# Slot tiles placed at multiples of 512 bytes in a decode kernel (attention over a long cache and an MLP)

## The chip, the cores and the metric

The kernel runs on one core of a Trainium2 chip. The metric is the device time of one execution in microseconds (us); the time before is a median of 404.12 us over three runs (403.59 to 404.19). The profile is that of one execution.

## What is computed

One token, a vector `x` of 1,024 numbers, goes through two branches that both start from the same layer norm; their results and `x` are added. Everything is bfloat16 in memory.

```python
xn = _layernorm(x)
return x + A(xn, k_cache, v_cache, wq, wo) + B(xn, w1, w2, w3, w4)

def A(x, k_cache, v_cache, wq, wo):        # caches: 4 heads x 65536 keys x 128
    q = (x @ wq) as 32 heads of 128        # 8 query heads share one cache head
    scores = q @ k.T * 128 ** -0.5
    return (softmax(scores) @ v) as one row @ wo

def B(x, w1, w2, w3, w4):
    h = gelu(layernorm(x) @ w1)
    hs = (h, each quarter shifted along the tokens) @ w2
    x1 = x + hs
    return x1 + gelu(layernorm(x1) @ w3) @ w4
```

With one token the shifted `h` is zero throughout, so that `x1` is `x`. The work is to read 134 MB of caches and 36 MB of weights once.

## The kernel before, in words

**Slots.** All the large data passes through three buffers of the pool `big` (L69, `SLOTS = 3`), each one tile `slot` of 128 partitions by 32,768 bf16 numbers, which is 65,536 bytes in each partition and 8.39 MB in all. The list `slots` (L112 to L123) sets the order of the stream: `wq`; then for each of the four cache heads `g` and each of its two blocks `t` one slot of keys (K) and one of values (V); `w3` behind the first V; a slot with `w1`, the first piece of `w4` and some gathered rows of `w4` ahead of the last head; `wo`; and last `w2` with the three remaining pieces of `w4` (`W4_PIECES = (13, 9, 3, 1)` rows a partition). So there are 21 slots of data for three buffers.

**The queue.** `issue` (L155) takes the next buffer and starts its transfers from SyncE (SP) at L169, one DMA for each piece. Each partition's part of a piece is contiguous both in HBM and in SBUF, so a DMA of a whole slot is 128 runs of 65,536 bytes, eight for each of 16 DMA engines. The main loop (L543) calls `ensure(i + LOOKAHEAD)` with `LOOKAHEAD = 2`: before slot `i` is worked on, slot `i + 2` is issued, which waits on SP until the buffer that it takes, that of slot `i - 1`, has been read for the last time. The gathered rows (L162 to L164) come through the GpSimd queue.

**Work on a slot.** A slot of keys (`compute_K`, L421) is done in two halves of 16,384 keys. For each half VectorE transposes the tile in place in four steps (L430, 128x2048 float32 words each), and TensorE multiplies it with the query held in `qst` (L434, 32 matmuls), followed by a running maximum (L438), the exponential (L457) and a transpose of the probabilities (L471). A slot of values (`compute_V`, L474) is 64 matmuls (L481) and two updates of the accumulator `og`. The weights go straight into matmuls of one row (L317, L525, L226). At the end ScalarE copies the sum `psB` out (L412), and SP writes it to HBM (L413).

**Where tiles lie in SBUF.** Pools lie one behind the other in the order in which they are opened (L66 to L71): `const`, `small`, `one`, `big`, `pp`, `tp`. Every tile is rounded up to 32 bytes. In the built program's table of allocations 16,384 bytes of each partition are reserved, four small constants follow, and `const` begins at byte 16,512. The three small pools take 9,664 bytes, so that the three slots begin at bytes 26,176, 91,712 and 157,248. Each of these is 64 more than a multiple of 512 (26,176 = 51 x 512 + 64). Pieces that share a slot begin at multiples of 2,048 bytes within it, so that every piece begins at 64 past a multiple of 512 too. `pp` begins at 222,784 and `tp` at 224,832. Among the tiles of `const` are `qst` and `eps_t`, the constant 1e-5 that the layer norm's square root takes as its bias (L201, L249).

Of the kernel before, what the change touches and what calls it, by code (L numbers as in the profile page):

```python
# [9 lines left out]
F32 = mybir.dt.float32  # L10
# [5 lines left out]
SLOTS = 3  # L16
# [7 lines left out]
XR = (4, 1)  # L24
XP = (((0, 12), (16, 20), (28, 44), (48, 52), (60, 68), (92, 100), (124, 128)), ((68, 84), (100, 116)))
NO_ROW = 4096


@with_exitstack
def kernel(  # L30
# [15 lines left out]
    P = 128  # L46
# [16 lines left out]
    assert FW <= 512 and F % 8 == 0  # L63
    SCALE = float(DH) ** -0.5

    const = ctx.enter_context(tc.tile_pool(name="const", bufs=1))  # L66
    small = ctx.enter_context(tc.tile_pool(name="small", bufs=2))
    one = ctx.enter_context(tc.tile_pool(name="one", bufs=1))
    big = ctx.enter_context(tc.tile_pool(name="big", bufs=SLOTS))  # L69
    ppool = ctx.enter_context(tc.tile_pool(name="pp", bufs=1))  # L70
    tpool = ctx.enter_context(tc.tile_pool(name="tp", bufs=2))  # L71
    dram = ctx.enter_context(tc.tile_pool(name="dram", bufs=1, space=bass.MemoryType.DRAM))
# [60 lines left out]
    def fill_x_row():  # L133
# [4 lines left out]
        for i, r in enumerate(XR):  # L138
            row, step = tmp(1), tmp(1)
            nc.vector.tensor_scalar(out=row, in0=pf, scalar1=float(x_start[i] // r + NO_ROW), scalar2=None, op0=ALU.add)  # L140
            end = 0
            for a, b in XP[i]:
                for t, jump in ((a, -NO_ROW - (a - end)), (b, NO_ROW)):
                    nc.vector.tensor_scalar(out=step, in0=pf, scalar1=float(t), scalar2=float(jump),
# [53 lines left out]
    make_identity(nc, ident_bf)  # L198
    ident_f = const.tile([P, P], F32, name="ident_f")
    make_identity(nc, ident_f[:])  # L200
    eps_t = const.tile([P, 1], F32, name="eps_t")  # L201
    nc.gpsimd.memset(eps_t[:], LN_EPS)
    ones_f = early[:, 64:192]
    nc.gpsimd.memset(ones_f, 1.0)
# [4 lines left out]
    def tmp(w):  # L209
        n_tmp[0] += w  # L210
        assert n_tmp[0] <= 512
        return early[:, n_tmp[0] - w:n_tmp[0]]
# [368 lines left out]
```

## Time and profile before

| | |
|---|---|
| median of three runs | 404.12 us (403.59 to 404.19) |
| profiled execution, its own time | 402.96 us |
| its span, from first to last instruction | 401.2 us |
| mean granted TensorE clock | 0.836 of full speed |
| busy: DMA queue of SP / VectorE / TensorE / ScalarE | 98% / 54% / 53% / 9% |
| bytes moved by DMA | 170.1 MB in the records, 170.67 MB read from HBM |

Busy time is the share of the span in which an engine ran instructions; for the DMA queue it is the time that its packets took, as a share of 16 engines' span. A *packet* is here one record of the trace, one contiguous run of bytes moved by one DMA engine. The profile's chain of waits follows the work that ended last back from the end: at each step to what released it. The groups give, for instructions of one kind, their number, total and mean duration, and the idle time of their engine ahead of them with the releaser. GB/s in the 40 slices of the span jumps between 410 and 460 because a packet's bytes are booked whole; the mean is what counts.

### The profile page before, as it was taken

The page shows a single profiled execution, that of the slowest core. Times are in us where ns is not written, and L with a number is a line of the kernel's source. Part 1 is how long each engine was busy: PE and PEld are TensorE (multiplying, and loading weights), DVE is VectorE, ACT ScalarE, POOL GpSimd, SP SyncE. Part 2 cuts the span into 40 slices and gives each one's busy share as a digit, 9 for nine tenths or more (in the row PEclk, how much of TensorE's full clock was granted, in tenths as well). Part 3 has the DMA queues.
Part 4 walks back from the last instruction along what each step waited for, and adds up shares of the span by engine and source line. Part 5 has one row for each costly group of instructions (what it writes and reads, how often), then busy time and mean ns, then how long its engine had stood idle before and what let it go on. Part 6 is the DMA issues. An engine that isn't in the chain of part 4 may idle for free.

```text
span 401.2 us, 3446 instructions
## 1 busy us (share of the span) xinstructions
PE 210.8 (53%) x1452; PEld 86.3 (22%) x1452; DVE 218.0 (54%) x291; ACT 35.7 (9%) x62; POOL 14.7 (4%) x24
## 2 busy tenths in 40 slices
PE   0003868540885196419662953385801965295763
PEld 0001323220332032104230411132400422031221
DVE  0006299501986498339845972696503982497300
ACT  0001000510012001100110011002200021001100
POOL 3000000002000000000000005100000000000000
PEclk9999969995798689958985999599865898599667
DMA  9999999999999999999999999999999999999985
GB/s 379 457 418 419 418 420 452 463 427 419 425 418 433 418 451 459 418 425 412 446 425 464 433 418 418 435 440 396 452 418 464 438 425 426 418 431 426 464 379 211
DMA packets 4234, 170.10 MB, mean 424 GB/s; under 512 B 936, under 2 KB 948, under 8 KB 1220
## 3 DMA queue, kind: packets, MB, share of 16 engines
q1 hardware_dynamic: 3608, 169.35, 98.0%
q0 software_dynamic: 416, 0.54, 0.4%
q8 instruction: 11, 0.18, 0.2%
q10 hardware_dynamic: 196, 0.00, 0.0%
q14 instruction: 3, 0.02, 0.0%
HBM read 170.67 MB, written 0.01 MB: 425 GB/s over the span
## 4 chain that ended last, share of the span: by engine, by line
DMA 54%; DVE 32%; PE 10%; another core or an unknown queue 2%; ACT 1%; ACTq 1%; issue 1%; SPq 0%; DVEq 0%
DMA slot<-in_A_k_cache_dram 38%; DVE slot L430 27%; DMA x_row_bf<-in_A_x_dram 9%; DMA slot<-in_B_w_dram 7%; PE oacc L481 4%; PE sc L434 3%; DVE mx L438 3%; PE rows L317 2%; DVE pT L471 1%; PE psB L226 1%; DVE og L489 1%; ACTq L180 1%; PE pm_mx L447 0%; DVE qst L330 0%
## 5 line engine op out<-in xcount | busy, mean ns | idle before, releaser
L434 PE MATMUL sc<-slot,qst 128*128 128x512 bf16 x512 | 133.7, 412 | 105.3 <-DVE slot L430 105.3
L430 DVE STREAM_TRANSPOSE slot<-slot 128x2048 f32<-128x2048 f32 x64 | 142.9, 2280 | 68.7 <-DMA slot<-in_A_k_cache_dram 68.6
L434 PEld LDWEIGHTS <-qst 128*128 128x128 bf16 x512 | 51.5, 103 | 175.6 <-DMA slot<-in_A_k_cache_dram 59.9
L481 PE MATMUL oacc<-slot,pT 128*32 128x512 bf16 x512 | 38.3, 452 | 6.8 <-DVE og L489 3.2
L457 ACT ACTIVATE p_sb<-sc,nm 128x1024 bf16<-128x1024 f32 x16 | 17.8, 1114 | 184.8 <-DVE nm L454 120.4
L471 DVE STREAM_TRANSPOSE pT<-p_sb 128x1024 bf16<-128x1024 bf16 x16 | 19.9, 1244 | 17.3 <-ACT p_sb L457 17.3
L438 DVE TENSOR_REDUCE mx<-sc 128x1 f32<-128x1024 f32 x16 | 19.2, 1203 | 4.5 <-PE sc L434 4.4
L481 PEld LDWEIGHTS <-pT 128*32 128x32 bf16 x512 | 14.8, 109 | 23.8 <-issue 12.0
L489 DVE SCALAR_TENSOR_TENSOR og<-og,alpha,oacc 128x512 f32<-128x512 f32 x12 | 8.8, 735 | 19.2 <-PE oacc L481 19.2
L238 PE MATMUL pm_ln<-early 128*128 128x1 f32 x4 | 1.1, 356 | 33.2 <-DVE early L274 30.7
L232 DVE CAST early<-x_bf 128x8 f32<-128x8 bf16 x1 | 0.2, 171 | 29.0 <-DMA x_bf<-in_A_x_dram 29.0
L440 PE MATMUL pm_mx<-ident_f,mx 128*1 128x128 f32 x16 | 4.3, 270 | 15.9 <-DVE mx L438 15.9
L457 ACT ACT_TABLE_LOAD x3 | 3.8, 1283 | 92.0 <-DVE nm L452 58.4
L162 POOL MEMSET slot<- 128x5120 bf16 x1 | 4.4, 4364 | 146.8 <-PE oacc L481 146.8
L238 PEld LDWEIGHTS pm_ln<-early 128*128 128x128 f32 x4 | 1.0, 313 | 33.2 <-issue 30.6
L447 PE MATMUL pm_mx<-ident_f,rep 1*128 1x1 f32 x16 | 3.6, 226 | 8.1 <-DVE rep L444 8.1
L525 PE MATMUL pm_w<-slot,oT 128*1 128x512 bf16 x64 | 5.7, 538 | 3.4 <-DMA slot<-in_A_wo_dram 3.4
L504 PE MATMUL pm_e<-og,sel8q 128*32 128x128 f32 x32 | 4.2, 276 | 5.0 <-DVE og L496 5.0
L317 PE MATMUL rows<-slot,early 128*32 128x512 bf16 x64 | 6.4, 589 | 0.0
L447 PEld LDWEIGHTS pm_mx<-ident_f,rep 1*128 1x128 f32 x16 | 2.3, 142 | 18.2 <-DVE rep L444 18.2
L440 PEld LDWEIGHTS pm_mx<-ident_f,mx 128*1 128x1 f32 x16 | 1.3, 79 | 21.3 <-DVE mx L438 20.4
L317 PE MATMUL rows<-slot,xpad 128*32 128x448 bf16 (+1 forms) x80 | 5.5, 358 | 0.0
(101 smaller groups left out, 95.4 us busy)
## 6 DMA issues: line engine op xcount, KB each, us to landing
slot<-in_B_w_dram SPq DMA_DIRECT2D x1, 7168.0 KB, 31.0
slot<-in_B_w_dram SPq DMA_DIRECT2D x2, 2048.0 KB, 28.4
slot<-in_B_w_dram SPq DMA_DIRECT2D x1, 3328.0 KB
slot<-in_B_w_dram SPq DMA_DIRECT2D x1, 2304.0 KB, 27.2
slot<-in_B_w_dram SPq DMA_DIRECT2D x1, 768.0 KB
slot<-in_B_w_dram SPq DMA_DIRECT2D x1, 256.0 KB
slot<-in_A_k_cache_dram SPq DMA_DIRECT2D x8, 48.2
slot<-in_A_v_cache_dram SPq DMA_DIRECT2D x8, 37.3
```

The costliest lines, as they stand in the source:

```text
L162: nc.gpsimd.memset(loaded[piece], 0.0)
L317: nc.tensor.matmul(acc[32 * j:32 * j + 32, bk, 0:width], lhsT=xp[:, c, :], rhs=wt[:, cl, ch * width:(ch + 1) * width], start=(c == 0), sto ...
L430: nc.vector.transpose(out=kf[:, cg, :], in_=kf[:, cg, :])
L434: nc.tensor.matmul(sc[:, hf, :], lhsT=qst[:, o:o + 128], rhs=kr[:, cg, hf, :, bp // 2, :, bp % 2], start=(cg == 0 and bp == 0), stop=(cg = ...
L438: nc.vector.reduce_max(out=mx[:], in_=sc[:].rearrange("p h n -> p (h n)"), axis=AX.X)
L440: nc.tensor.transpose(pm[0:1, 0:P], mx[:, 0:1], ident_f[:])
L447: nc.tensor.transpose(pm[:, P:P + 1], rep[0:1, :], ident_f[0:1, 0:1])
L457: nc.scalar.activation(out=p_sb[:], in_=sc[:], func=ACTF.Exp, bias=nm[:, 0:1], scale=SCALE, accum_out=lb[:, 0:1])
L471: nc.vector.transpose(out=pT[:], in_=p_sb[:])
L481: nc.tensor.matmul(oacc[32 * u:32 * (u + 1), :], lhsT=pT[:, hf, 32 * t:32 * (t + 1)], rhs=vt[:, :, hf, t, :], start=(hf == 0 and t < 4), s ...
L489: nc.vector.scalar_tensor_tensor(out=st["og"][:], in0=st["og"][:], scalar=alpha[:, 0:1], in1=oacc[:], op0=ALU.mult, op1=ALU.add)
L525: nc.tensor.matmul(psW[32 * q:32 * q + 1, :], lhsT=lhsT, rhs=wrow[:, 512 * b:512 * b + 512], start=(i < 2), stop=(i >= n - 2), tile_positi ...
```

## The change

Two pools are opened ahead of `const`: a new pool `head` with a single tile, and the pool `big`, which stood behind `one`. The tile in `head` is 96 float32 numbers, 384 bytes in a partition; its first number takes the part of `eps_t`, which leaves `const`. With that the tile begins at byte 16,512 = 32 x 512 + 128, and the first slot 384 bytes later, at 16,896 = 33 x 512. As a slot is 128 x 512 bytes, the other two begin at multiples of 512 as well (82,432 and 147,968), and so does every piece in them. The small pools follow at 213,504 = 417 x 512. As `eps_t` with its 32 bytes is gone from `const`, the tiles behind it move by 32 bytes against their pool's start: `qst`, which began at a multiple of 64, begins at 32 past one, and so do the tiles of `pp` and `tp` (now from 223,136 and 225,184).

No instruction is added, removed or given another shape, and the order in which they are issued stays.

```diff
+HEAD = 96
...
+    head = ctx.enter_context(tc.tile_pool(name="head", bufs=1))
+    big = ctx.enter_context(tc.tile_pool(name="big", bufs=SLOTS))
     const = ctx.enter_context(tc.tile_pool(name="const", bufs=1))
     small = ctx.enter_context(tc.tile_pool(name="small", bufs=2))
     one = ctx.enter_context(tc.tile_pool(name="one", bufs=1))
-    big = ctx.enter_context(tc.tile_pool(name="big", bufs=SLOTS))
...
-    eps_t = const.tile([P, 1], F32, name="eps_t")
+    eps_t = head.tile([P, HEAD], F32, name="eps_t")[:, 0:1]
     nc.gpsimd.memset(eps_t[:], LN_EPS)
```

## The prediction

> **What bounds the kernel now.** I read the page's head first: the span, the DMA row of the 40 slices, and the queues.
>
> ```profile
> span 401.2 us, 3446 instructions
> ...
> DMA  9999999999999999999999999999999999999985
> ...
> DMA packets 4234, 170.10 MB, mean 424 GB/s; under 512 B 936, under 2 KB 948, under 8 KB 1220
> ...
> q1 hardware_dynamic: 3608, 169.35, 98.0%
> ```
>
> The 16 DMA engines are at work from the first slice to the next to last, and one queue, SP's, holds 98.0% of their time. No other engine comes near (VectorE 54%, TensorE 53%). The chain of waits seems to say something else:
>
> ```profile
> DMA 54%; DVE 32%; PE 10%; another core or an unknown queue 2%; ACT 1%; ACTq 1%; issue 1%; SPq 0%; DVEq 0%
> DMA slot<-in_A_k_cache_dram 38%; DVE slot L430 27%; DMA x_row_bf<-in_A_x_dram 9%; DMA slot<-in_B_w_dram 7%; PE oacc L481 4%; PE sc L434 3%; DVE mx L438 3%; PE rows L317 2%; DVE pT L471 1%; PE psB L226 1%; DVE og L489 1%; ACTq L180 1%; PE pm_mx L447 0%; DVE qst L330 0%
> ```
>
> VectorE's transposes (L430) have 27% of it. They are there because the chain steps from a landing back to its issue, and an issue waits for a buffer. Whether that delays anything shows in the third view, the issues of a slot by time, against when the queue ran dry:
>
> ```profile
> 48.74 0.33 SPq L169 DMA_DIRECT2D slot<-in_B_w_dram  x1
> 73.57 0.33 SPq L169 DMA_DIRECT2D slot<-in_A_k_cache_dram  x1
> 81.42 0.33 SPq L169 DMA_DIRECT2D slot<-in_A_v_cache_dram  x1
> ```
>
> A slot takes 8.39 MB / 433 GB/s = 19.4 us to move, and the rows of the tile `slot` give 37.1 us from issue to landing in the median, so it stands in the queue behind another for some 18 us. The tightest issue is the one at 73.57: in the packet records the slot ahead of it (`w3`) ends at 77.44 on its first engine, and the first packet of the run came 1.03 us after its issue (0.75 to 1.78). That leaves 77.44 - 73.57 - 1.03 = **2.8 us of cover**. By the same reckoning the other issues that wait for a buffer have over 7 us. So the stream never runs dry, and the time is what the packets take.
>
> The packet records of SP's queue, by size (each is one run in one partition), show what that is:
>
> ```
> bytes    packets  median ns   at 32 B per 1.1765 ns   left over ns
> 65,536     2304     2420            2409.4               10.6
> 57,344      128     2116            2108.2                7.8
> 26,624      128      989             978.8               10.2
> 18,432      128      688             677.6               10.4
> 16,384      256      614             602.4               11.6
>  6,144      128      236             225.9               10.1
>  2,048      128       84              75.3                8.7
>      4      404        9               0.1                8.9
> ```
>
> From 2,048 to 65,536 bytes it is 2,336 ns for 63,488 bytes: 27.2 bytes in a ns, or 32 bytes each 1.1765 ns, and a fixed part of about 9 ns a packet. 94.9% of the 2,304 large ones lie within 2,415 to 2,430 ns. The time adds up from that: for each engine 144 x 2.420 + 8 x (2.116 + 0.989 + 0.688 + 0.236 + 0.084) + 16 x 0.614 = 348.5 + 32.9 + 9.8 = 391.2 us; 0.7 us more, since the first 16 took 3.1 us instead of 2.4; gathers 1.5 and instruction loads 1.0 (the other queues' packet time over 16 engines, partly beside the others). That is 394.4 of the 395.5 us from the first packet (1.78) to the last (397.32). Ahead lie 1.8 us, behind it 3.9 us (16 matmuls into `psB`, L412, the output). Span 401.2, own time 402.96, which is 1.16 us under the median of 404.12. I work out differences on the former and put them on the median.
>
> **The change part by part.** *The slots' start*, 64 past a multiple of 512 before, at one after. It can touch the packets' time in two places. The part that grows with the bytes: an unaligned start that cost something at each 256 or 512 bytes would show in the slope. [...] Cost: 0. [...] The nearest row is that of 4 bytes, the completion writes, which move no data and go to no slot: 9 ns as well. So the fixed part is there without a slot, and I take a saving of **0 ns**. Bounds: at best the whole left-over, 8.7 ns by the slope, goes. An engine has 144 + 40 + 16 = 200 packets, so that is 200 x 8.7 = 1.74 us: 404.12 - 1.74 = 402.4. At worst a packet gets longer; the only other duration seen at this size, besides the first 16 and those shared with an instruction load, is a band of about 2,480 ns (61 packets between 36 and 301 us), 60 ns more: 144 x 0.060 = 8.6 us, 412.8. The value is near the 4-byte row, and so zero.
>
> [...]
>
> *VectorE and TensorE on a slot.* L430 takes 2,267 to 2,312 ns in all 64 cases and in three buffers; L434 376 in the least and 377 in the median. I cost them at nothing, since the words, steps and order stay; if they change, the cover is the 2.8 us above in one place and over 7 us elsewhere. *The small tiles' shift by 32 bytes* (`qst` as weights of L434, 96 ns each in the median; `p_sb`, `pT`, `og`): under the same cover, except ahead of the first issue and in the last 3.9 us. There the 16 matmuls of L226 (1.02 us) read a slot, the ACT copy 0.37 us; a tenth of these is 0.14 us, under what can be seen. *`eps_t`*: the same memset of one column (0.09 us on POOL at 1.62), needed by L249 more than 30 us later. The SP queue gets the same 26 issues. Sum: **0 us, 404.1**.
>
> **Rivals.** *The whole fixed part goes* (or more than 4.0 ns of it, the point at which 200 packets make 0.81 us, 0.2%): 402.4. For it: the left-over of about 10 ns stands in every size of slot packet. Against: 9 ns stand at 4 bytes too.
>
> [...]
>
> *Slower, by a slower in-place transpose.* If L430 gets slower on a tile at the new place, the eight on the first K slot end later, and with them the issue at 73.57. Up to 2.8 us are covered, so it decides from 2.8 / 8 = 0.35 us a transpose (15%); at 20% (0.45 us) 3.6 - 2.8 = 0.8 us are lost, and at 30% 2.6 us: 404.9 to 406.7, middle 405.2. Against: its narrow spread over three buffers, and that the new start is the rounder one.
>
> *Slower, by longer packets*: from 4.0 ns a packet on; 412.8 if all took the 2,480 ns that the band shows. Against: the band holds 61 packets of 2,304 with the same start as the others.
>
> *It doesn't do what it says*: the starts are worked out from the pools' sizes and could not be missed without another order of pools; 404.1 as well.
>
> **How the numbers follow.** A change within 0.2% (0.81 us) can hardly be told from none with this kernel. Nothing happens, or the slots don't move: 0.55. Two steps a packet: 0.12. Both are within 0.2%: same 0.67. The whole fixed part or most of it: 0.18, faster. A slower transpose 0.07 and longer packets 0.08: slower 0.15. The likeliest is 404.1. The range goes from 402.3, the full fixed part with 0.1 us for the spread, to 405.3, the transposes' middle; beyond it stay most of the longer packets and the far end of the transposes, about 0.1.
>
> **What would show it.** In the packet records after, 65,536 bytes at 2,418 to 2,420 ns again: nothing gained. At 2,411: the rival with the whole fixed part. [...] The sum over the queue stays at 169.35 MB and its share at 98%. The issue behind `w3` should stay at 73.6 and the L430 row at 2,271 ns in the median; an issue behind 76.4 means the slower transpose. The prediction is wrong if the slope itself changes: a slot packet well under 2,409 ns would say that 32 bytes each 1.1765 ns was the limit of the unaligned start and not of the engines.

## The result, and the profile after

The changed kernel takes **402.52 us** in the median of seven runs (402.29 to 403.13); the kernel before, run beside it, 404.12 (403.59 to 405.64, seven runs). The ratio is 0.9959, with a 95% interval of 0.9942 to 0.9976. So it became faster by 0.4%, where no change was forecast; the time lies in the forecast range, near its lower end.

The profiled execution after took 402.46 us with a span of 400.7 us, 0.5 us less than the one of before. The page after, with its head, queue and the chain's shares:

```profile
span 400.7 us, 3446 instructions
...
DMA  9999999999999999999999999999999999999994
...
DMA packets 4234, 170.10 MB, mean 425 GB/s; under 512 B 936, under 2 KB 948, under 8 KB 1220
...
q1 hardware_dynamic: 3608, 169.35, 97.9%
...
DMA 54%; DVE 32%; PE 10%; another core or an unknown queue 2%; ACT 1%; ACTq 1%; issue 1%; SPq 0%; DVEq 0%
DMA slot<-in_A_k_cache_dram 37%; DVE slot L434 27%; DMA x_row_bf<-in_A_x_dram 9%; DMA slot<-in_B_w_dram 7%; PE oacc L485 4%; PE sc L438 3%; DVE mx L442 3%; PE rows L321 2%; DVE pT L475 1%; PE psB L230 1%; DVE og L493 1%; ACTq L184 1%; PE pm_mx L451 0%; DVE qst L334 0%
```

(Lines of the file after are four higher: L434 is the transpose that was L430, L173 the issue that was L169.) The same packets and bytes flow, and DMA is still the bound; a page of rounded shares can't show a change of 0.4% spread over the whole stream. VectorE's row and the issues behind the first K slot:

```profile
L434 DVE STREAM_TRANSPOSE slot<-slot x64: 2268/2270/2312, 52.4 to 362.8; 128x2048 f32<-128x2048 f32 x64
```

```profile
73.60 0.33 SPq L173 DMA_DIRECT2D slot<-in_A_k_cache_dram  x1
81.46 0.33 SPq L173 DMA_DIRECT2D slot<-in_A_v_cache_dram  x1
```

The transposes are as they were, within 1 ns (2267/2271/2312 before), and the tight issue stands at 73.60, where it was 73.57. So the transposes and the tight issue did not move. The packet records of SP's queue show what did. Here are the 2,288 packets of 65,536 bytes behind the first 16, by duration in ns:

```
             2,418 or less   2,419-2,423   2,424-2,430   2,431-2,500   longer
before              549          1085           552            90         12
after              2170            46            21            34         17
```

and the share that took exactly 2,418 ns, by the time of their start in us:

```
            4-20   20-40   40-60   60-100   100-140   140-200   200-260   330-400
before       90%     96%     94%      29%       17%        6%        5%        6%
after        87%     99%     88%      72%       92%       98%       98%       99%
```

The unaligned kernel begins like the aligned one. Between 60 and 140 us its packets go over into a pattern that repeats along each engine (2,420, 2,420, 2,420, 2,427, 2,420, 2,418, 2,427 and so on) and stay in it. The aligned one has some long packets in the same stretch and then comes back to 2,418. The time of the packets that fill slots, over 16 engines, falls from 392.83 to 392.12 us, 0.50 of it in the large packets and 0.21 in the smaller ones.

### The profile page after: what moved, and what is told of

Read it like the earlier page. It is cut to its first block, busy times and chain, and to the rows that moved or that the text cites. A ratio compares the mean times of both kernels' runs of the same rounds, so it can differ in the third digit from the quotient of the medians.

```text
span 400.7 us, 3446 instructions
## 1 busy us (share of the span) xinstructions
PE 214.7 (54%) x1452; PEld 86.8 (22%) x1452; DVE 218.0 (54%) x291; ACT 35.7 (9%) x62; POOL 14.7 (4%) x24
## 3 DMA queue, kind: packets, MB, share of 16 engines
q1 hardware_dynamic: 3608, 169.35, 97.9%
## 4 chain that ended last, share of the span: by engine, by line
DMA 54%; DVE 32%; PE 10%; another core or an unknown queue 2%; ACT 1%; ACTq 1%; issue 1%; SPq 0%; DVEq 0%
DMA slot<-in_A_k_cache_dram 37%; DVE slot L434 27%; DMA x_row_bf<-in_A_x_dram 9%; DMA slot<-in_B_w_dram 7%; PE oacc L485 4%; PE sc L438 3%; DVE mx L442 3%; PE rows L321 2%; DVE pT L475 1%; PE psB L230 1%; DVE og L493 1%; ACTq L184 1%; PE pm_mx L451 0%; DVE qst L334 0%
## 5 line engine op out<-in xcount | busy, mean ns | idle before, releaser
L434 DVE STREAM_TRANSPOSE slot<-slot 128x2048 f32<-128x2048 f32 x64 | 142.9, 2280 | 64.4 <-DMA slot<-in_A_k_cache_dram 64.4
L485 PE MATMUL oacc<-slot,pT 128*32 128x512 bf16 x512 | 41.9, 485 | 6.6 <-DVE og L493 3.2
L485 PEld LDWEIGHTS <-pT 128*32 128x32 bf16 x512 | 15.7, 115 | 25.8 <-issue 16.6
```

What stands on the lines that cost most here:

```text
L434: nc.vector.transpose(out=kf[:, cg, :], in_=kf[:, cg, :])
L485: nc.tensor.matmul(oacc[32 * u:32 * (u + 1), :], lhsT=pT[:, hf, 32 * t:32 * (t + 1)], rhs=vt[:, :, hf, t, :], start=(hf == 0 and t < 4), s ...
```

## The experiments

**Order of the pools, or start of the slots.** e1 keeps the old order and moves two tiles of 32 bytes behind the slots; e2 keeps the new order and puts the slots back to 64 past 512; e3 and e4 put them at 256 and 32.

```diff
 # e1, from the kernel before
     big = ctx.enter_context(tc.tile_pool(name="big", bufs=SLOTS))
+    late = ctx.enter_context(tc.tile_pool(name="late", bufs=2))
...
-            ls = small.tile([P, 1], F32, name="ls")
+            ls = late.tile([P, 1], F32, name="ls")
```

> Pool order as before; one small tile pair of 64 bytes goes behind the slots, so that these begin 64 bytes lower, at multiples of 512; `const`, `small`, `pp` and `tp` stay where they were before. If the slots' start makes the difference: 402.5 us, ratio to before 0.996, packets of 65,536 bytes at 2,418 ns for nearly all of the run. If it is the order of the pools or the new places of the small tiles: as before, 404.1 us, packets in the uneven pattern of 2,418 to 2,427 ns.

```diff
 # e2, from the changed kernel
-HEAD = 96
+HEAD = 112
```

> Pool order of the changed kernel, but with 448 bytes ahead of the slots, so that they begin at 64 past a multiple of 512 as before the change. If the slots' start makes the difference: 404.1 us, ratio 1.000, packets uneven. If the order or the small tiles make it: 402.5, ratio 0.996, packets at 2,418 ns.

```diff
 # e3, from the changed kernel
-HEAD = 96
+HEAD = 32
```

> Pool order of the changed kernel with 128 bytes ahead of the slots: they begin at 256 past a multiple of 512. If a start at a multiple of 256 is enough: 402.5, ratio 0.996, packets at 2,418 ns. If only 512 does it: 404.1, ratio 1.000, packets uneven.

```diff
 # e4, from the changed kernel
-HEAD = 96
+HEAD = 104
```

> Pool order of the changed kernel with 416 bytes ahead of the slots: they begin at 32 past a multiple of 512. If the loss at 64 came from steps of 64 bytes being whole, this one is slower than before: over 404.5, ratio over 1.001. If any start off 512 (or 256) costs the same: 404.1, ratio 1.000. If the slots' start doesn't matter: 402.5, ratio 0.996.

Then, as the limit lay between 64 and 256, e8 with the slots at 128, and e7, the kernel before once more for a second profile:

```diff
 # e8, from the changed kernel
-    head = ctx.enter_context(tc.tile_pool(name="head", bufs=1))
     big = ctx.enter_context(tc.tile_pool(name="big", bufs=SLOTS))
...
-    eps_t = head.tile([P, HEAD], F32, name="eps_t")[:, 0:1]
+    eps_t = const.tile([P, 1], F32, name="eps_t")
```

> Pool order of the changed kernel without any bytes ahead of the slots (`eps_t` is back in `const`): they begin at 128 past a multiple of 512. At 256 and 0 the packets' time over 16 engines was 392.1 to 392.2 us, at 64 392.8, at 32 393.0. If a start at a multiple of 256 is what counts: 392.7 to 392.8 us, time near 403.6, ratio to before 1.000. If a multiple of 128 is enough: 392.1, time 402.5, ratio 0.997.

```diff
 # e7, from the kernel before
+# before, once more
```

> The kernel before, unchanged, for a second profile. If the place is all: 403.6 us (402.9 to 405.4 were measured), packets in the same uneven pattern from the fourth slot on, and the sum of the packets' time over 16 engines at 392.8 us or more. If the pattern of the first profile was chance, the packets are at 2,418 ns throughout.

What was measured. "Packet" is the mean of the 65,536-byte packets that start from 205 to 235 us (about 200, one lengthened by an instruction load in each kernel), "at 2,418" the share of them that took exactly 2,418 ns; "sum" is the time of the packets that fill slots over 16 engines, "engines' end" the mean time at which the 16 engines finished the last slot. A ratio is to the kernel before as run beside that kernel on the same chip (403.62 us in the median for e1, e2, e3 and e4, 403.51 for e8), so it can differ from the ratio of two rows of the table.

```
kernel   slots at   order  packet ns  at 2,418   sum us  engines' end  span us  median us  ratio to before (95%)
before   512n+64     old    2424.4       5%      392.83     396.70      401.2    404.12
e7       512n+64     old    2424.5       5%      392.78     396.99      401.4    403.16 (one run)
e2       512n+64     new    2424.4       5%      392.81     396.81      401.2    403.60    0.9995 (0.9981-1.0008)
e8       512n+128    new    2424.3      15%      392.65     396.91      401.6    403.69    1.0000 (0.9984-1.0016)
e4       512n+32     new    2425.3       0%      393.03     396.95      401.5    403.90    1.0001 (0.9985-1.0016)
after    512n        new    2420.6      99%      392.12     395.90      400.7    402.52    0.9959 (0.9942-0.9976)
e1       512n        old    2420.6      99%      392.12     396.11      400.7    402.62    0.9970 (0.9954-0.9986)
e3       512n+256    new    2421.8      92%      392.17     395.98      400.1    402.53    0.9965 (0.9950-0.9979)
```

The spans and transposes of the pages of e1 and of e2, which differ in order and start:

```profile
span 400.7 us, 3446 instructions
...
L431 DVE STREAM_TRANSPOSE slot<-slot 128x2048 f32<-128x2048 f32 x64 | 142.9, 2280 | 66.1 <-DMA slot<-in_A_k_cache_dram 66.0
```

```profile
span 401.2 us, 3446 instructions
...
L434 DVE STREAM_TRANSPOSE slot<-slot 128x2048 f32<-128x2048 f32 x64 | 142.9, 2280 | 61.7 <-DMA slot<-in_A_k_cache_dram 61.7
```

The order of the pools did nothing here: with it and the old start, e2 is as the kernel before (ratio 0.9995); without it and with the new start, e1 is as the kernel after (0.9970). VectorE's work on a slot is 142.9 us in both. The start decides, and 256 was enough (0.9965) while 128 wasn't (1.0000): the intervals of the three kernels at multiples of 256 lie below 1, those of the three others hold 1. e4 at 32 was expected to be slower than before if a step of 64 mattered; its packets are 0.9 ns longer than those at 64, but its time can't be told from theirs. A start at 256 isn't quite as quiet as one at 512: without the lengthened packet the mean in e3 is 2,419.3 ns against 2,418.0 in the changed kernel. A few of its engines leave 2,418 for some packets and come back; from 330 us on 99% are at 2,418.

**A cost for each packet, or a share of the bytes.** e5 (slots at 64) and e6 (slots at 0) load each K and V slot in eight DMAs, each with an eighth of every partition's run. e5 has the old order of the pools and e6 the new one, which e1 and e2 showed to make no difference:

```diff
-            nc.sync.dma_start(out=t[:, at:at + w], in_=src)
+            cut = 4096 if piece[0] in ("K", "V") else w
+            for c in range(0, w, cut):
+                nc.sync.dma_start(out=t[:, at + c:at + c + cut], in_=src[:, c:c + cut])
```

> The kernel before (slots at 64 past a multiple of 512), with every K and V slot loaded by eight DMAs of 8,192 bytes a partition in place of one of 65,536, so that an engine has 1,024 packets for the caches in place of 128. If a start off 256 costs about 3.6 ns for each packet whatever its length, the loss against the same cut at aligned starts grows to 896 x 3.6 = 3 us and more beside the 0.6 us. If it is a share of the bytes' time, it stays at 0.6 to 1.1 us. The cut alone costs 896 x 9 ns = 8 us by the fixed part of a packet, so about 412 us here.

> The changed kernel (slots at multiples of 512) with the same cut into eight DMAs a K or V slot. With 896 packets more at about 9 ns: 402.5 + 8 = 410.5 us. If the loss at 64 is one for each packet, this is 3.6 us or more under its twin at 64; if it goes with the bytes, 0.6 to 1.1 us under it.

The span and queue of e5, then of e6:

```profile
span 409.8 us, 3583 instructions
...
DMA packets 20363, 170.12 MB, mean 415 GB/s; under 512 B 2728, under 2 KB 2740, under 8 KB 3012
...
q1 hardware_dynamic: 19736, 169.36, 98.9%
```

```profile
span 404.8 us, 3583 instructions
...
DMA packets 20363, 170.12 MB, mean 420 GB/s; under 512 B 2728, under 2 KB 2740, under 8 KB 3012
...
q1 hardware_dynamic: 19736, 169.36, 98.8%
```

Same bytes, same packets, 5.0 us apart. The medians are 411.87 us (ratio to before 1.0199, 1.0174 to 1.0224) and 407.34 (1.0085, 1.0061 to 1.011), 4.5 us apart, against 1.0 to 1.6 without the cut. The 16,384 packets of 8,192 bytes take 314.0 ns in the mean at 64 and 309.3 at 0: 4.7 ns x 1,024 on each engine = 4.8 us. So the loss is one of the packet, not of the byte: 4.7 ns on a packet of 8,192 bytes here, 3.8 on one of 65,536 above (2,424.4 against 2,420.6). The cut by itself was dearer in the forecast than on the chip: e6 is 4.8 us over the changed kernel, 5.4 ns for each of the 896 packets more, not 9. By duration a packet more is 8.1 ns ((8 x 309.3 - 2,418) / 7). But strung together by their times into 16 engines, the records of e6 overlap: nearly every packet starts 3 or 4 ns before the one ahead of it ends, which leaves about 5 ns of the engine's time.

**What starts the pattern.** In the traces of before, e2 and e4 some engines left 2,418 right behind a packet that an instruction load had lengthened by about 500 ns (to 2,874 to 3,080 in before), and I took interruption by another queue for the start. To test that, a load stream alone, with nothing on TensorE. This is its loop; each tile `slot` begins at a multiple of 512 bytes, and `OFF` counts bf16 numbers of 2 bytes:

```python
for g in range(4):
    for t in range(2):
        for cache in (A_k_cache, A_v_cache):
            s = big.tile([P, SLOT + 256], BF16, name="slot")
            src = cache[0, g, t * 32768:(t + 1) * 32768, :].rearrange("(p k) d -> p (k d)", p=P)
            nc.sync.dma_start(out=s[:, OFF:OFF + SLOT], in_=src)
            nc.vector.tensor_copy(out=o[0:1, n:n + 1], in_=s[0:1, OFF:OFF + 1])
            if n in TINY:
                nc.scalar.copy(out=x[0:1, 0:1], in_=s[0:1, OFF:OFF + 1])
                nc.scalar.dma_start(out=x[:, 0:8], in_=A_x[0, 0, :].rearrange("(p c) -> p c", c=8))
                nc.scalar.copy(out=o[0:1, 512 + n:513 + n], in_=x[0:1, 0:1])
            n += 1
```

```diff
 # s2: 64 bytes off, no small DMA
+OFF = 32
+TINY = ()
```

> A load stream alone: the 16 slots of the K and V caches, 128 packets of 65,536 bytes each, through three buffers, each read by one element's copy; all of the attention, the weights and the MLP are left out. The data begins 64 past a multiple of 512; no other DMA runs beside it, but for what loads of instructions there are. If a start off 256 costs something only after an engine was interrupted by another queue: nearly all packets at 2,418 ns. If it costs something in itself: the uneven pattern from the start, mean 2,422 or more.

```diff
 # s3: 64 bytes off
+OFF = 32
+TINY = (3,)
```

> The same stream at 64, with one small DMA (128 runs of 16 bytes) from ScalarE's queue behind the landing of the fourth slot. By the interruption theory: 2,418 ns up to it, and from then on in every engine the uneven pattern, mean 2,421 to 2,422. If it costs something in itself: uneven ahead of the small DMA as well. If the pattern needs more than a small DMA (load on VectorE or TensorE): 2,418 ns throughout.

```diff
 # s4: aligned
+OFF = 0
+TINY = (3,)
```

> The same stream with the small DMA, data at a multiple of 512. By the interruption theory as by the other: 2,418 ns throughout, but for the packets that share the engine with the small ones.

```diff
 # s6: 16 bytes off
+OFF = 8
+TINY = (3,)
```

> [...] If only interruptions matter: 2,418 ns ahead of the small DMA and uneven behind it, about as at 32 and 64. [...]

The mean of the 65,536-byte packets in ns, by time in us, and the share at 2,418:

```
                     20-40         80-100        140-160       180-200       220-240       260-280
s2 (64, quiet)    2420.1  48%   2475.7  13%   2418.0 100%   2418.1  96%   2421.8   3%   2422.0   9%
s3 (64)           2419.6  56%   2419.1  84%   2421.3   8%   2422.1   9%   2421.6   2%   2421.8  10%
s4 (0)            2419.7  56%   2480.7  30%   2418.0 100%   2418.0 100%   2418.0 100%   2418.0 100%
s6 (16)           2421.9  58%   2424.7  65%   2422.2  22%   2423.9   0%   2423.4   0%   2423.7   0%
```

The page of s2 shows which queues were at work:

```profile
DMA packets 2306, 134.22 MB, mean 425 GB/s; under 512 B 257, under 2 KB 257, under 8 KB 258
...
q1 hardware_dynamic: 2306, 134.22, 98.6%
```

and that of s4:

```profile
DMA packets 2450, 134.22 MB, mean 425 GB/s; under 512 B 401, under 2 KB 401, under 8 KB 402
...
q1 hardware_dynamic: 2306, 134.22, 98.5%
q10 hardware_dynamic: 144, 0.00, 0.0%
```

My theory fell. In s2 no other queue moved a packet after the stream had begun, and yet all 16 engines went over into the pattern, between 190 and 210 us, after 70 us at a clean 2,418. In s3 the small DMA (queue q10) ran from 87 to 104 us, and the engines went over one by one, most between about 95 and 135 and the last at about 165; in s6 most did between 115 and 150. s4 came back to 2,418 and stayed there, in spite of the same small DMA. So the pattern set in sooner or later in every traced run with a start off a multiple of 256, and in none with a start at one. It came latest in e8 with the slots at 128, where 22% of the packets still took 2,418 ns from 200 to 260 us. The pattern needs neither the work of TensorE, nor the transposes of VectorE, nor another queue. That a small DMA brings it on sooner isn't excluded: the engines of s3 and s6 went over earlier than those of s2, in one execution each. What makes it set in at one time or another is open. Once in it, a packet took 3.8 ns more at 64 (2,421.8 against 2,418.0, from 260 to 280 us) and 5.7 more at 16 (2,423.7), so the start at 16 cost 1.9 ns more than the one at 64.

## Why the prediction was right or wrong

*The bound* was right: the DMA queue is busy from end to end (98.0% before, 97.9% after; a slot's 19.4 us are eight packets of 2,420 ns on each engine), the issue at 73.6 kept its cover, and the time moved with the packets while the transposes, 27% of the chain, stayed as they were.

*The part that grows with the bytes* was taken as nothing, which was my estimate: no record of before shows it. The runs did. From 2,048 to 65,536 bytes the medians differ by 2,334 ns after and by 2,336 before, and e5 and e6 show a loss for each packet.

*The fixed part, "a saving of 0 ns" from the 4-byte row,* is the step that failed. The reasoning went from a median and a fixed part of about 9 ns that the 404 packets of 4 bytes have too. That fixed part is real and stayed: after the change it is 9 ns at 4 bytes and 84 ns at 2,048 bytes as before, and 2,418 ns at 65,536. But the unaligned start adds to it on top, unevenly, 0 to 9 ns with 3.8 in the mean. I had read "94.9% lie within 2,415 to 2,430 ns" as agreement, when 10 ns in 2,420 are 0.4%, the whole size of the question. The trace of before held the answer: its own packets ran at 2,418 for the first 60 us and at more for the rest. A floor that the same kernel reaches at one time and misses at another points at a loss that may be removed, and here it was. The prediction's sum hid it as well: made with medians it gives 391.9 us for the packets that fill slots (391.2 + 0.7), where the records themselves hold 392.83.

*Two steps a packet,* with a chance of 0.12: no run shows a step of 32 bytes, or that two of them are lost. The records show a rate, 27.2 bytes in a ns, and the runs show a loss once a packet at 64: 4.7 ns at 8,192 bytes (e5 and e6), 3.8 at 65,536, and 0.7 us in the packets' sum (392.8 to 392.1). What lengthens a packet isn't shown. It isn't there from the first packet on, as the unaligned kernel had 90 to 96% of its packets at 2,418 ns for some 60 us. The sign set down for nothing gained, 2,418 to 2,420 ns again, came although 1.6 us were gained: the median went from 2,420 to 2,418. Of the six smaller sizes four became 2 to 3 ns shorter, while 57,344 and 2,048 bytes stayed. A start at 256 was enough, one at 128 wasn't (402.53 and 403.69 us). Packets were longer than the aligned ones by 5.7 ns at 16 (in the stream), 4.7 at 32, 3.8 at 64 and 3.7 at 128, so of these four starts the one nearest behind a multiple of 256 cost most.

*The rival of the whole fixed part* gave 402.4 and the result is 402.52, but not for its reason; the fixed part is still there (9 ns at 4 bytes). That rival also set the lower end of the range, 402.3, and so it is luck that the measured time lies within it: the forecast itself, no change or one within 0.2%, did not come.

*The slower transpose and the longer packets* didn't come; L434 is at 2,270 ns and 2,170 of 2,288 packets at 2,418 or less.

*The size.* The packets' sum explains 0.7 us. The engines finish the last slot 0.6 to 1.1 us earlier in the three kernels at multiples of 256 than in the five others (395.9 to 396.1 against 396.7 to 397.0); the spans differ by 0.9 us in the mean (400.5 against 401.4). In the medians it is about 1.1 us (402.5 to 402.6 against 403.5 to 404.2), and 1.6 in the first comparison. The profiled executions of the unaligned kernels lie in the lower part of their own runs (402.96 us for the kernel before, where 33 runs gave 402.9 to 405.4 with a median of 403.62); what the longer runs hold beyond the pattern stays open.

## What to carry to other kernels

Where a stream of DMAs sets the time, try a start of every run in SBUF at a multiple of 256 bytes: it costs some padding and gave 0.3 to 0.4% here with runs of 65,536 bytes (the table's ratios), and 4.5 of 412 us with runs of 8,192. To see whether a kernel has that to gain, don't take the median of its packets' durations; look at their distribution and at their course over the run, for a loss that sets in once and stays. And judge a spread by the effect that is asked for: 10 ns of 2,420 looked like nothing, and they held the 3.8 ns a packet that the change won.

## What the runs showed beyond that

A second disturbance comes with either start. Between 80 and 100 us the packets of s2 and s4 took 2,476 and 2,481 ns in the mean, 2.4 to 2.6% more, those of s3 2,419, with the same stream. These are single executions, and what brings it on in one and not in another is open. The packets' sum over 16 engines is 311.2 us in s2, 310.9 in s4 and 310.5 in s3, so that s3 at 64 was faster (316.93 us) than s4 aligned (317.48). The 0.7 us between s2 and s3, both at 64, are as much as the change takes off the packets' sum, and one time of each stream would have given the wrong sign.
